# Two of three convolution taps on GpSimd, V shifted by DMA, and loads issued from two queues

## The chip, the cores and the metric

The kernel runs on one core of one Trainium2 chip. The metric is the device time of one execution in microseconds (us), as the median of several runs. The engines are TensorE (PE in the profile, with its weight loads as PEld), VectorE (DVE), ScalarE (ACT), GpSimd (POOL) and SyncE (SP, which here only issues DMAs). Each engine works through its own instructions in a fixed order.

## The reference

Sliding-window attention over 8 batches of 8 heads, 576 positions and 64 elements, then a feed-forward part with a gated three-tap convolution along the sequence:

```python
def _attn_ref(q, k, v):                       # B=8, H=8, S=576, D=64
    scores = scale * np.matmul(q, k.transpose(0, 1, 3, 2))
    mask = np.abs(pos[:, None] - pos[None, :]) <= 32
    ...                                       # masked softmax
    return np.matmul(attn, v)

def _moe_ref(x, w_in, conv_w, w_out):         # d_model=512, d_ff=1024
    h = np.maximum(x @ w_in, 0.0)
    ...                                       # hp: h padded by one row at each end
    for k in range(3):
        conv_out += conv_w[k][None, None, :] * hp[:, k:k + S, :]
    gate = 1.0 / (1.0 + np.exp(-conv_out))
    return h * gate @ w_out
```

## The kernel before

The rows of all batches are cut into 12 chunks of 384 and the 1024 hidden features into 8 blocks of 128. One (chunk, block) pair is a unit: a projection into PSUM on TensorE, ReLU on ScalarE, three convolution taps, tanh on ScalarE, the gate on VectorE. A tap on TensorE is a matmul with a diagonal matrix; in 79 units the middle tap is instead multiplied and added into PSUM by VectorE.

```python
        on_dve = m < P["tap"][c]
        kks = (0, 2) if on_dve else (0, 1, 2)

        def emit_pc(e_):
            for kk in kks:
                tensor.matmul(pc.ap[:, 0:nc_], diag_w[:, kk, m, :], taps(kk), start=(kk == 0), stop=(kk == 2))
# ... cut ...
            def emit_tap(e_):
                vector.scalar_tensor_tensor(
                    out=in3(pc.ap), in0=taps(1), scalar=conv_w_sb[:, 1, m:m + 1], in1=in3(pc.ap),
                    op0=ALU.mult, op1=ALU.add,
                )
```

All large loads are issued by SyncE: four query and key loads of 576 KB per batch (two groups of heads each), five V loads of 192 or 256 KB, and two loads for each weight matrix.

```python
        def emit(e):                                   # load_qk
            src = (q, k)[y][b, 4 * i:4 * i + 4, :, :]
            sync.dma_start(
                s.ap[:, y].rearrange("p e j d -> p e (j d)"),
                bass.AP(src.tensor, src.offset, [[RP * D, 128], [2 * S * D, 2], [1, RP * D]]),
            )
# ... cut ...
        def emit_hi(e):                                # shift_v: V moved by 64 rows, on VectorE
            mover(e, vo[0:64, c0:c1], ve[64:128, c0:c1])
```

The order of instructions on each engine is not written by hand. The program holds a planner: it simulates the engines with given costs and given priorities (the dictionary `P`, found by a search over many plans) and emits each engine's instructions in the order that its simulation gives. So the times in `P` fit one plan, and a part moved by hand leaves every other instruction where the plan had put it.

The softmax here doesn't subtract the row's maximum and nothing guards it: scores larger than these inputs give would overflow.

## Time and profile before

| | before |
|---|---|
| time, median of the 3 runs | 236.06 us (234.93 to 236.89) |
| span of the profiled execution | 234.2 us |
| first projection matmul starts | 24.6 us |
| from there to the end | 209.6 us |
| TensorE, VectorE, ScalarE, GpSimd busy | 219.8, 197.5, 181.6, 62.8 us |

I take as the end of the start the first matmul of the projection `pf<-xT,w_in_sb`, because from there the feed-forward work can fill TensorE. The view of the tile w_in_sb gives it; its columns are shortest, median and longest duration in ns, then the start of the first and of the last.

```profile
L380 PE MATMUL pf<-xT,w_in_sb x416: 243/327/338, 24.6 to 223.4; 128*128 128x385 bf16 x88, 128*128 128x386 bf16 x30, 128*128 128x193 bf16 x21
```

The window of the first 24 us (window, length, busy time and count of PE, PEld, DVE, ACT and POOL, granted clock, DMA share, GB/s) shows DMA engines nearly full:

```profile
0.00:24.00 24.00, 18.06 (x301) 12.38 (x302) 17.89 (x60) 16.09 (x41) 10.81 (x40) 1.00 0.98 295
```

### The profile page before, as it was taken

The numbers are of one execution on the slowest core, as the hardware profiler recorded it, in microseconds if no ns is written. First come the engines' busy times: TensorE is split into PE (matmuls) and PEld (weight loads), VectorE is DVE, ScalarE is ACT, GpSimd is POOL, SyncE is SP. The second block draws the span as 40 slices with busy tenths as digits, with TensorE's granted clock in tenths as the row PEclk, the third lists the DMA queues.
The fourth block names the chain that finished last, engine by engine and source line by source line (L and its number), as shares of the span: only waits on it lengthen the run. The fifth ranks groups of instructions, "written<-read, shape, count | busy, mean of one in ns | idle before, by whom it ended". The sixth has DMA issues, their size and how long they took to land.

```text
span 234.2 us, 7175 instructions
## 1 busy us (share of the span) xinstructions
PE 219.8 (94%) x2790; PEld 128.5 (55%) x2790; DVE 197.5 (84%) x463; ACT 181.6 (78%) x432; POOL 62.8 (27%) x101
## 2 busy tenths in 40 slices
PE   7777999899999899999999999999999999999992
PEld 4555556578555555655555555555555655555550
DVE  6489989896999999999999999887997995867271
ACT  3796989999999697798689687797599855766361
POOL 4336655552733531152360210340000000000000
PEclk9999999999999999999999999999999999999999
DMA  6999999999999988649995994981442143211204
GB/s 219 294 261 393 284 264 299 359 201 379 201 321 326 243 273 242 153 55 264 372 196 60 253 186 119 328 219 46 69 75 99 48 88 102 92 45 45 91 3 179
DMA packets 66054, 45.37 MB, mean 194 GB/s; under 512 B 51148, under 2 KB 51172, under 8 KB 66020
## 3 DMA queue, kind: packets, MB, share of 16 engines
q1 hardware_dynamic: 65984, 44.90, 71.1%
q8 instruction: 22, 0.36, 0.8%
q14 instruction: 12, 0.10, 0.1%
q10 hardware_dynamic: 36, 0.01, 0.0%
HBM read 32.52 MB, written 9.44 MB: 179 GB/s over the span
## 4 chain that ended last, share of the span: by engine, by line
PE 65%; DVE 19%; ACT 5%; DMA 3%; issue 3%; SPq 1%; ACTq 0%; POOL 0%; DVEq 0%; POOLq 0%
PE pf L380 65%; DVE gT L380 5%; DVE attn L380 4%; DMA vst<-in_v_dram 3%; DVE pf L380 3%; DVE diag_w L380 3%; ACT attn L380 2%; DVE vo L380 2%; DVE xn L380 1%; SPq L380 1%; ACT pf L380 1%; ACT xn L380 1%; DVE rec L380 1%; DVE qkT L380 1%; DVE xT L380 1%
## 5 line engine op out<-in xcount | busy, mean ns | idle before, releaser
L380 PE MATMUL pf<-xT,w_in_sb 128*128 128x385 bf16 (+2 forms) x416 | 73.9, 315 | 1.4 <-DVE gT L380 0.9
L380 PE MATMUL pf<-w_out_sb,gT 128*128 128x512 bf16 x288 | 67.8, 379 | 0.1
L380 ACT ACTIVATE pf<-pf 128x384 f32<-128x384 f32 (+1 forms) x104 | 47.0, 478 | 13.1 <-DVE pf L380 12.3
L380 ACT ACTIVATE hT<-pf 128x385 bf16<-128x385 f32 (+2 forms) x104 | 48.1, 501 | 11.3 <-PE pf L380 10.1
L380 DVE SCALAR_TENSOR_TENSOR gT<-pf,hT 128x384 bf16<-128x384 f32 (+1 forms) x104 | 51.4, 519 | 5.9 <-ACT pf L380 5.3
L380 DVE SCALAR_TENSOR_TENSOR pf<-hT,conv_w_sb,pf 128x384 f32<-128x384 bf16 x79 | 46.0, 616 | 11.4 <-PE pf L380 10.3
L380 PEld LDWEIGHTS <-w_in_sb 128*128 128x128 bf16 x416 | 38.8, 98 | 24.9 <-issue 2.7
L380 PE MATMUL pf<-hT,diag_w 128*128 128x384 bf16 (+1 forms) x233 | 46.3, 310 | 0.7 <-DVE gT L380 0.3
L380 POOL TENSOR_SCALAR qkb<-st 128x1152 bf16<-128x1152 f32 (+1 forms) x27 | 29.6, 1097 | 57.2 <-DMA st<-in_q_dram 30.5
L380 PEld LDWEIGHTS <-gT 128*128 128x128 bf16 x288 | 27.4, 98 | 29.7 <-ACT attn L380 0.3
L380 ACT ACTIVATE attn<-pf 128x512 bf16<-128x512 f32 (+1 forms) x96 | 41.0, 528 | 2.1 <-PE pf L380 1.9
L380 POOL TENSOR_SCALAR ve<-vst 128x512 bf16<-128x512 f32 x37 | 25.0, 682 | 30.4 <-DMA vst<-in_v_dram 24.6
L380 DVE TENSOR_TENSOR attn<-attn,mask 128x1152 bf16<-128x1152 bf16 x32 | 27.5, 859 | 5.2 <-ACT attn L380 4.8
L380 ACT COPY y<-pf 128x512 f32<-128x512 f32 x32 | 19.5, 612 | 11.1 <-PE pf L380 7.4
L380 PEld LDWEIGHTS <-diag_w 128*128 128x128 bf16 x233 | 19.8, 97 | 13.2 <-issue 0.8
L380 ACT COPY qkT<-pf 128x576 bf16<-128x576 bf16 x36 | 22.7, 660 | 1.8 <-PE pf L380 1.7
L380 DVE TENSOR_TENSOR xn<-pf,rec 128x256 bf16<-128x256 f32 x64 | 23.4, 408 | 0.1
L380 DVE COPY qkT<-pf 128x576 bf16<-128x576 bf16 x28 | 20.4, 748 | 2.9 <-PE pf L380 2.3
L380 DVE COPY vo<-ve 64x520 bf16<-64x520 bf16 (+1 forms) x28 | 15.4, 549 | 2.0 <-POOL ve L380 1.2
L380 PEld LDWEIGHTS <-attn 128*64 128x64 bf16 x576 | 11.8, 110 | 9.4 <-issue 5.7
L380 PE MATMUL pf<-ve,attn 128*64 128x65 bf16 x320 | 15.0, 197 | 2.1 <-DVE attn L380 1.2
L380 PE MATMUL pf<-qkT 64*128 64x64 bf16 x576 | 14.3, 191 | 1.6 <-DVE qkT L380 0.9
(39 smaller groups left out, 139.4 us busy)
## 6 DMA issues: line engine op xcount, KB each, us to landing
st<-in_q_dram SPq DMA_DIRECT2D x16, 576.0 KB, 6.7
st<-in_k_dram SPq DMA_DIRECT2D x16, 576.0 KB, 7.2
out_dram<-y SPq DMA_DIRECT2D x36, 256.0 KB, 2.4
vst<-in_v_dram SPq DMA_DIRECT2D x24, 256.0 KB, 8.5
vst<-in_v_dram SPq DMA_DIRECT2D x16, 192.0 KB, 7.5
st<-in_moe_w_in_dram SPq DMA_DIRECT2D x2, 1024.0 KB, 7.1
st<-in_moe_w_out_dram SPq DMA_DIRECT2D x2, 1024.0 KB, 7.8
xT<-xn SPq DMA_TRANSPOSE x30, 2.5
```

The source lines that it names most:

```text
L380: return lambda *args, **kwargs: fixed(do(*args, **kwargs))
```

## The change

The intent is to relieve TensorE, which is busy 94% of the span: in some units no tap is left on it, GpSimd makes two of them in fp32 SBUF, and VectorE adds the third and writes PSUM. To pay for this, VectorE loses its large V shifts to DMA, and GpSimd loses the query and key casts of batches 2 to 7. The query and key loads of batches 0 and 1 go to ScalarE's queue, beside SyncE's. The planner gets a model of two queues, and all of `P` is searched anew. The core of the diff, with cuts:

```diff
+    PLANS = {
+        "3": ((0, 1, 2), (), ()), "2": ((0, 2), (), (1,)), "1": ((0,), (), (1, 2)),
+        "q": ((), (0, 2), (1,)), "r": ((), (0,), (1, 2)), "s": ((0,), (1, 2), ()),
+    }                                        # taps on TensorE, on GpSimd, on VectorE
 ...
+        def emit_mul(e_, cp, kk):
+            gpsimd.tensor_scalar(
+                out=in3(cp.ap), in0=taps(kk), scalar1=w_tap(kk), scalar2=0.0, op0=ALU.mult, op1=ALU.add
+            )
+        def emit_add(e_):
+            gpsimd.tensor_tensor(out=in3(cps[0].ap), in0=in3(cps[0].ap), in1=in3(cps[1].ap), op=ALU.add)
 ...
+        def emit_tap(e_, kk, from_):
+            vector.scalar_tensor_tensor(
+                out=in3(pc.ap), in0=taps(kk), scalar=w_tap(kk), in1=in3(from_.ap), op0=ALU.mult, op1=ALU.add,
+            )
 ...
+    queue = {"SP": sync, "ACT": scalar}
-            sync.dma_start(
+            queue[e].dma_start(              # in every load; also in mover, for the shift of V
 ...
- 'e_vo': (('DVE',), ('DVE',), ('DVE',)),
+ 'e_vo': (('DVE',), ('DVE',), ('SP',)),
- 'e_qk': (('POOL', 'DVE', 'ACT'), ('POOL',), ('POOL', 'ACT')),
+ 'e_qk': (('POOL', 'ACT'), ('POOL', 'DVE', 'ACT'), ('DVE', 'ACT')),
+ 'q_qk': ('ACT', 'ACT', 'SP'),
+ 'q_v': (('SP', 'SP', 'SP', 'SP', 'SP'), ('SP', 'SP', 'SP', 'SP', 'ACT'), 'SP'),
+ 'q_w_in': 'SP',
+ 'kind': ('33333333', '33333333', '2q222222', '22qq2q2q', '22qq212q', '2q2q2222', 'q2222q22', '2qsq222q', '222q2q2q',
+          'qs222q22', '22q12q2q', 'q2sr2q2q'),
```

## The prediction

> **What bounds the kernel now.** I read the page's shares first, then the chain that ended last, then busy time by stage, then the groups of instructions with what they waited for. The page:
>
> ```profile
> PE 219.8 (94%) x2790; PEld 128.5 (55%) x2790; DVE 197.5 (84%) x463; ACT 181.6 (78%) x432; POOL 62.8 (27%) x101
> ...
> PE 65%; DVE 19%; ACT 5%; DMA 3%; issue 3%; SPq 1%; ACTq 0%; POOL 0%; DVEq 0%; POOLq 0%
> ```
>
> TensorE is busy 94% and carries 65% of the chain that ended last; VectorE carries 19%; GpSimd, idle for 73% of the span, none. The chain in order of time shows where: its late part is one unbroken TensorE piece.
>
> ```profile
> 3.60 7.82 DMA vst<-in_v_dram
> ...
> 24.21 5.16 DVE diag_w L380 x15
> 29.89 9.18 PE pf L380 x167
> ...
> 145.21 15.12 PE pf L380 x189
> 160.35 0.60 ACT attn L380
> 160.95 0.38 ACT pf L380
> 161.33 0.52 ACT attn L380
> 161.85 0.04 issue
> 161.90 67.35 PE pf L380 x589
> ```
>
> So there are three stages: a start that waits for loads and then for VectorE (to about 24 us), a middle in which TensorE and VectorE alternate in the chain, and from about 145 us a stage that TensorE alone sets. Busy time in the last two:
>
> ```profile
> 24.00:150.00 126.00, 122.19 (x1730) 73.20 (x1729) 117.09 (x272) 108.21 (x263) 48.78 (x56) 1.00 0.93 242
> 150.00:229.00 79.00, 78.91 (x761) 42.84 (x759) 61.80 (x132) 56.24 (x127) 3.21 (x5) 1.00 0.31 85
> ```
>
> The columns are window, length, then busy time (and count) of PE, PEld, DVE, ACT and POOL, granted clock, DMA share, GB/s. In the middle VectorE is at 117.1/126 = 93%, almost as full as TensorE. In the last stage TensorE has 78.9 of 79 us, VectorE 78%, ScalarE 71%, GpSimd 4%. That contrast decides my numbers: a TensorE instruction saved late is worth its full time, one saved in the middle only a part.
>
> The groups that the change touches:
>
> ```profile
> L380 PE MATMUL pf<-hT,diag_w 128*128 128x384 bf16 (+1 forms) x233 | 46.3, 310 | 0.7 <-DVE gT L380 0.3
> L380 DVE SCALAR_TENSOR_TENSOR pf<-hT,conv_w_sb,pf 128x384 f32<-128x384 bf16 x79 | 46.0, 616 | 11.4 <-PE pf L380 10.3
> L380 POOL TENSOR_SCALAR qkb<-st 128x1152 bf16<-128x1152 f32 (+1 forms) x27 | 29.6, 1097 | 57.2 <-DMA st<-in_q_dram 30.5
> L380 DVE COPY vo<-ve 64x520 bf16<-64x520 bf16 (+1 forms) x28 | 15.4, 549 | 2.0 <-POOL ve L380 1.2
> ```
>
> The first is the convolution on TensorE: 233 diagonal matmuls. The second is the middle tap, which 79 units already leave to VectorE. The 310 ns of one matmul is latency, not cost: in the timeline five of them begin at 183.43 us and the next operation at 184.25 us, so one costs 0.82/5 = 0.164 us of TensorE.
>
> **What the Trainium skill says.** "TensorE: Matmul & The Clock Gate", the section "Wait — 56ns, not 53.3ns?", gives start to start as N/2.4 GHz plus about 2.5 ns; for 384 columns that is 0.1625 us, and the trace's 0.164 agrees. "GPSIMD Engine Reference", section 3.1, gives about 2.6 cycles per element for a two-input operation at 1.2 GHz and about one for a light one-input body. The trace has no two-input GpSimd operation; its one-input casts agree (1152 elements 1.151 us, 512 elements 0.621 us by their medians: 0.83 ns, one cycle, per element, and 0.2 us fixed). "SBUF — State Buffer", the section "SBUF: two separate sides", says that VectorE and GpSimd share a port pair under an exclusive lock, for VectorE operations with two SBUF inputs or in a 2-port mode. The trace agrees in kind: the mask multiply takes 0.758 us in the median and 1.484 at most, the shift copies of V stretch to 1.533. "DMA: Bandwidth & Descriptors", the section "Issuing engines are not separate DMA queues", says that a second issuing engine saves only issue time; this trace, with nearly all traffic on one queue, can't show it.
>
> **The change part by part.** The new plan string gives each unit of chunks 2 to 11 a kind. I count 26 q (two taps on GpSimd, none on TensorE), 3 s (one tap on TensorE, two on GpSimd, a plain add on VectorE), 1 r (one tap on GpSimd, two on VectorE), 2 "1" (one on TensorE, two on VectorE) and 48 "2", the present split; chunks 0 and 1 keep three taps on TensorE.
>
> TensorE. Those 80 units use 48*2 + 2*1 + 3*1 = 101 matmuls, against 79*2 + 3 = 161 now. Sixty go: 60 * 0.164 = 9.8 us. By chunk 2 to 11 the sixty lie 2, 8, 7, 4, 4, 7, 7, 5, 7, 9. The last stage begins with some 5.3 chunks left (42 of VectorE's gate operations lie in it, 8 to a chunk), so about 36 of the sixty fall in it: 5.9 us. The other 24 are in the middle: 3.9 us.
>
> GpSimd. A multiply of 384 elements by the casts' line is 0.2 + 384*0.83 ns = 0.52 us; an add, estimated from the skill's 2.6 cycles, 0.2 + 384*2.17 ns = 1.03 us. A q or s unit costs 2*0.52 + 1.03 = 2.07 us; 29 of them and one lone multiply make 60.6 us. From it go the query and key casts of batches 2 to 7, no longer allowed there: about 20 of the 23 large ones at 1.15 us, 23 us. GpSimd ends near 62.8 + 60.6 - 23 = 100 us, under half the span.
>
> VectorE. In a q unit one operation (middle tap plus GpSimd's sum, into PSUM) replaces the present tap, and in an s unit a plain add does: I count both as 0.616 us, no change. The r, the two "1" and the one unit that had three TensorE taps add about four operations, 2.5 us. The 12 large shift copies of batches 2 to 7 become DMAs: minus 12 * 0.795 (the large form's mean) = 9.5 us. Against that, the 24 casts of batches 2 to 7 now go to VectorE or ScalarE. Split evenly, that is 12 on ScalarE at 1.16 us (its mean for this form), 14 us, of which some 6 are there already, and 12 on VectorE at, as an estimate from the mask's 0.726 us best case for the same length, 0.7 us: 8.4 us. ScalarE does eight normalizations of the first batches in 32 pieces; in batch 0 they may now go to VectorE only, at most eight times 0.41 = 3.3 us. The sum is +4.7 us, to about 202, before locks. Those are the sore point: GpSimd now reads SBUF in the late stage as well, and some 85 VectorE operations (32 masks, 29 new taps, a dozen casts, remaining shifts) can meet it. With GpSimd busy 45% and a mean remainder of 0.4 us, an unplanned meeting costs 0.18 us on average, up to 15 us in all; the schedule plans around part of it. I take 6 us, giving about 208.
>
> Start. Query and key loads of batches 0 and 1 go to ScalarE's queue while V stays on SyncE's. Now SyncE is held 8.33 us issuing the first five V loads, and the chain runs through them (7.82 us). But DMA engines are 98% busy in the first 24 us, so the second queue reorders bytes more than it adds any. I give it 0.
>
> The sum: late stage 5.9 us, of which I keep 5.2 (locks and thinner slack cost a little); middle 3.9 us, of which I keep 2.1, because VectorE there loses shifts but gains casts and meetings; start 0. 236.06 - 7.3 = 228.8 us, 3.1% less.
>
> **The rivals.** First, *VectorE takes TensorE's place.* At 208 of 229 us it would be 91% busy, and in the middle it is at 93% already. For it: 19% of the chain is VectorE today, and ScalarE already waits 12.3 us for the taps. Against it: the late stage has 17 us of VectorE slack in 79. If only the late gain survives, 231 us; if meetings cost all that I feared, 233 to 235.
>
> Second, *GpSimd's latency becomes a wait.* A q unit's chain after its ReLU grows by 2.07 us, with two scratch buffers, one unit ahead at best, and the in-order GpSimd queue also holds V casts that wait for their loads (24.6 us of such waits now). A late load then holds up a tap, a tanh and a gate. For it: every queue has a fixed order. Against it: most waiting before V casts lies in the middle, 3.3 us of it after 150. It would cost 2 to 4 us: 231 to 233.
>
> Third, *all of it is kept.* The two queues smooth the loads, shifts leave VectorE's critical moments, and the whole 9.8 us plus 1 to 3 us at the start come out: 223 to 226 us. For it: the entire schedule was retuned with the change. Against it: the tail of about 5 us after the last matmul and DMA-bound start stay.
>
> **Range and chances.** 228.8 us is the sum above; 224.5 is the third rival's middle, 233.5 the first's worse half. The 2% line is 231.3 us, 2.5 us above my figure, and the late gain alone nearly reaches it. Faster by over 2%: 0.69; within 2%: 0.28; slower by over 2%: 0.03.
>
> **What would show it.** Diagonal matmuls should number 173, and TensorE's busy time fall to about 206 to 211 us. GpSimd should be near 100 us with some 59 multiplies of 0.5 us and 29 adds of 1.0 us; no large shift copy on VectorE; V shifts as twelve DMAs; casts of queries on VectorE or ScalarE after batch 1. If VectorE carries clearly over 19% of the chain, or its two-SBUF-input operations grow well past their medians, the first rival has it; if taps wait for GpSimd by many microseconds, the second. My prediction is wrong if the span after 150 us shrinks by less than 4 us, or if the start changes by more than 2 us either way.

## More of the kernel before

ScalarE's timeline at the start follows: start, duration, engine, instruction, and in brackets the idle time before it and what ended it. ACTq is the issue of a DMA.

```profile
0.80 0.65 ACTq L380 DMA_DIRECT2D conv_w<-in_moe_conv_w_dram  x1
1.48 1.28 ACT L380 ACT_TABLE_LOAD   x1 [1.48 <-PEq L1010]
5.02 0.73 ACT L380 CAST qkb<-st 128x640 bf16<-128x640 f32 x1 [2.27 <-DMA st<-in_q_dram]
```

ScalarE issues one small load, loads its table, and casts the first query at 5.02 us, as soon as it has landed.

## The result, and the profile after

The changed kernel takes 243.44 us (median of four runs, 241.67 to 244.91); the kernel before, beside it, 235.68 us (four runs). The ratio is 1.0321, with a 95% interval of 1.0235 to 1.0408: slower, where I had predicted 228.8 us. A ratio here is the mean time of one kernel's fast runs over that of the other's in the same rounds, so it is not quite the ratio of the medians quoted beside it. Executions over 1.5% slower than the fastest of the same kernel are left out of the means.

The page of the changed kernel, busy times and chain:

```profile
PE 213.7 (88%) x2692; PEld 125.6 (52%) x2715; DVE 192.9 (80%) x475; ACT 190.0 (78%) x427; POOL 101.9 (42%) x160
...
PE 39%; DVE 23%; ACT 20%; DMA 7%; issue 6%; POOL 2%; SPq 0%; ACTq 0%; DVEq 0%; POOLq 0%
```

TensorE and VectorE both have less work than before, and yet the span is 8.1 us longer. TensorE's share of the chain fell from 65% to 39%, while VectorE's rose from 19% to 23% and ScalarE's from 5% to 20%. The tile view says where it begins:

```profile
L445 PE MATMUL pf<-xT,w_in_sb x416: 244/327/338, 38.6 to 229.7; 128*128 128x385 bf16 x88, 128*128 128x386 bf16 x30, 128*128 128x193 bf16 x21
```

The first projection starts at 38.6 us instead of 24.6, 14.0 us later. The windows from there to the end, before and then after:

```profile
24.60:234.20 209.60, 201.26 (x2485) 115.83 (x2484) 178.98 (x402) 164.92 (x391) 51.62 (x61) 1.00 0.69 182
```

```profile
38.60:242.30 203.70, 189.76 (x2260) 109.72 (x2281) 170.08 (x401) 168.95 (x388) 83.84 (x113) 0.99 0.70 183
38.60:166.00 127.40, 119.93 (x1613) 71.73 (x1625) 109.89 (x270) 115.47 (x269) 43.98 (x61) 0.99 0.89 232
166.00:234.00 68.00, 66.92 (x637) 36.87 (x646) 58.94 (x130) 52.17 (x118) 39.87 (x52) 1.00 0.38 102
```

So the start is 14.0 us longer, the rest 209.6 - 203.7 = 5.9 us shorter, and 14.0 - 5.9 = 8.1. TensorE's busy time in the rest fell by 11.5 us, at nearly the same clock. The last two lines answer to the prediction's middle and late stage: TensorE still fills the late one (66.9 of 68 us), VectorE is at 87% in it where it was at 78%, and GpSimd at 59% where it was at 4%.

These two numbers are not a pure loss and a pure gain, because the mark cuts the work at different places. The windows of TensorE's score matmuls, which read the tile qkT, from 0 to the first projection (before, then after; busy time and count, clock, DMA share, GB/s):

```profile
0.00:24.60 24.60, 1.79 (x72) 1.00 0.99 297
0.00:38.60 38.60, 4.76 (x144) 0.78 0.96 291
```

One batch has 576/8 = 72 of them. The transposes of queries and keys stand at 72 and 144 as well. So the new plan puts the front of batch 1's attention, 144 matmuls, ahead of the first projection: that work has moved from the rest into the start. At full clock it keeps TensorE busy some 5.9 us (10.2 us for both groups in run b below against 4.3 in run d, which has them once).

What the parts of the change became stands in the groups of instructions of the changed kernel (busy us and mean ns of one after the bar, then idle time before them and what ended it):

```profile
L445 POOL TENSOR_SCALAR cp<-hT,conv_w_sb 128x384 f32<-128x384 bf16 x59 | 39.1, 672 | 56.5 <-ACT hT L445 43.2
...
L445 PE MATMUL pf<-hT,diag_w 128*128 128x384 bf16 (+1 forms) x173 | 34.1, 306 | 3.6 <-ACT hT L445 2.6
...
L445 POOL TENSOR_TENSOR cp<-cp,cp 128x384 f32<-128x384 f32 x29 | 28.9, 998 | 2.0
...
L445 DVE TENSOR_TENSOR attn<-attn,mask 128x1152 bf16<-128x1152 bf16 x32 | 24.8, 777 | 1.6 <-ACT attn L445 1.6
...
L445 DVE SCALAR_TENSOR_TENSOR pf<-hT,conv_w_sb,cp 128x384 f32<-128x384 bf16 x27 | 17.4, 644 | 6.2 <-POOL cp L445 3.1
```

There are 173 diagonal matmuls, 59 multiplies and 29 adds, as counted from the plan string. VectorE's taps that read GpSimd's sum waited only 3.1 us for it. The mask multiply, which has two SBUF inputs and can meet GpSimd, takes 777 ns in the mean.

The start is read from ScalarE's timeline in the changed kernel:

```profile
1.45 0.41 ACTq L445 DMA_DIRECT2D st<-in_q_dram  x1
...
3.12 0.99 ACTq L445 DMA_DIRECT2D st<-in_k_dram  x1
7.50 0.38 ACTq L445 DMA_DIRECT2D st<-in_q_dram  x1
7.91 0.48 ACTq L445 DMA_DIRECT2D st<-in_k_dram  x1
9.36 0.38 ACTq L445 DMA_DIRECT2D st<-in_q_dram  x1
13.21 0.37 ACTq L445 DMA_DIRECT2D st<-in_k_dram  x1
13.62 1.28 ACT L445 ACT_TABLE_LOAD   x1 [13.62 <-DMA vst<-in_v_dram]
14.91 0.62 ACT L445 CAST qkb<-st 128x512 bf16<-128x512 f32 x1
```

The first four loads (batch 0) go out in 0.4 to 1.0 us each. The next four (batch 1) go out at 7.50, 7.91, 9.36 and 13.21 us, and each of the gaps ends when an earlier load has landed: GpSimd's casts of batch 0's first query and key, which wait for their loads, start at 7.56 and 9.42 us, and the chain has a V load under way from 1.84 us for 11.35 us, to 13.19. In the program's own instruction list these issues carry a wait: every load counts up one of eight completion counters, taken in turn by the loads of both queues, and a load waits until the eighth load before it has landed. ScalarE executes in order, so these waits hold back its computing too: its first cast runs at 14.91 us and not at 5.02. The list of waits has it in two places, first the hold, then TensorE behind the cast:

```profile
ACT L445 <- DMA vst<-in_v_dram: 13.6, 1, 13.6
...
PE pf L445 <- ACT qkb L445: 10.4, 1, 10.4
```

The columns are the total, the number of times and the longest wait. The second queue moved no more bytes: in the same first 24 us as above the transfer rate is 292 GB/s, against 295, while every engine did about half to four fifths of the work.

```profile
0.00:24.00 24.00, 11.99 (x162) 7.53 (x163) 9.35 (x40) 8.63 (x15) 9.12 (x34) 0.72 0.93 292
```

SyncE's timeline of the changed kernel shows the third thing: with batch 1's queries and keys already under way, w_in is issued at 17.61 us, where the kernel before, which sends w_in ahead of batch 1, issues it at 11.98.

### The profile page after: what moved, and what is told of

Same layout as the page of the kernel before. It is cut to its first block, busy times and chain, and to the rows that moved or that the text cites.

```text
span 242.3 us, 7092 instructions
## 1 busy us (share of the span) xinstructions
PE 213.7 (88%) x2692; PEld 125.6 (52%) x2715; DVE 192.9 (80%) x475; ACT 190.0 (78%) x427; POOL 101.9 (42%) x160
## 4 chain that ended last, share of the span: by engine, by line
PE 39%; DVE 23%; ACT 20%; DMA 7%; issue 6%; POOL 2%; SPq 0%; ACTq 0%; DVEq 0%; POOLq 0%
PE pf L445 39%; DMA vst<-in_v_dram 7%; ACT attn L445 6%; DVE pf L445 5%; DVE gT L445 4%; ACT hT L445 4%; ACT pf L445 4%; DVE attn L445 4%; DVE xn L445 3%; ACT qkT L445 3%; DVE qkT L445 2%; DVE vo L445 2%; POOL cp L445 2%; ACT y L445 1%; DVE rec L445 1%
## 5 line engine op out<-in xcount | busy, mean ns | idle before, releaser
L445 POOL TENSOR_SCALAR cp<-hT,conv_w_sb 128x384 f32<-128x384 bf16 x59 | 39.1, 672 | 56.5 <-ACT hT L445 43.2
L445 POOL TENSOR_SCALAR ve<-vst 128x512 bf16<-128x512 f32 x31 | 20.2, 657 | 55.2 <-DMA vst<-in_v_dram 28.2
L445 PE MATMUL pf<-hT,diag_w 128*128 128x384 bf16 (+1 forms) x173 | 34.1, 306 | 3.6 <-ACT hT L445 2.6
L445 DVE SCALAR_TENSOR_TENSOR pf<-hT,conv_w_sb,pf 128x384 f32<-128x384 bf16 x53 | 31.5, 616 | 6.4 <-PE pf L445 5.3
L445 POOL TENSOR_TENSOR cp<-cp,cp 128x384 f32<-128x384 f32 x29 | 28.9, 998 | 2.0
L445 ACT COPY qkT<-pf 128x576 bf16<-128x576 bf16 x39 | 25.4, 710 | 1.8 <-PE pf L445 1.8
L445 DVE TENSOR_TENSOR xn<-pf,rec 128x256 bf16<-128x256 f32 x69 | 25.2, 410 | 0.1
L445 PE MATMUL pf<-ident,qkb 64*128 64x64 bf16 x576 | 14.4, 195 | 10.6 <-ACT qkb L445 10.4
L445 ACT CAST qkb<-st 128x1152 bf16<-128x1152 f32 (+2 forms) x21 | 23.1, 1109 | 0.0
L445 DVE SCALAR_TENSOR_TENSOR pf<-hT,conv_w_sb,cp 128x384 f32<-128x384 bf16 x27 | 17.4, 644 | 6.2 <-POOL cp L445 3.1
L445 PEld LDWEIGHTS <-diag_w 128*128 128x128 bf16 x173 | 14.8, 97 | 12.3 <-issue 3.5
```

Source lines behind the costliest of these rows:

```text
L445: return lambda *args, **kwargs: fixed(do(*args, **kwargs))
```

## The experiments

**Theory 1**, at first: ScalarE's held-up computing is the cost of the start (most of the 14 us), and undoing it gives the time back. **Rival 1**: two queues share the same DMA engines, so every urgent load lands later, whoever issues it. **Rival 2**: the order of the bytes is the cost, batch 1's four loads (4 * 576 KB = 2.36 MB) ahead of V's last blocks and of w_in; at 295 GB/s they are worth some 8 us, as an estimate from the window above. All twelve kernels gave correct results. The ratios and medians use fast runs alone; slow ones were one of six of h, one of four of k, one of 17 of l, and four of the 11 of the kernel before beside h, i and j. The fast median of the kernel before, run beside each, was 235.56 us for a to d, 234.56 for e to g, 234.58 for h to j, 234.69 for k and 234.76 for l. The table gives for each profiled execution the two parts of the span, and how many matmuls of batch 1's attention (transposes and scores) stand ahead of the first projection.

| run | first projection, us | batch 1's matmuls ahead | from there to the end, us | median us | ratio to before (95%) |
|---|---|---|---|---|---|
| before | 24.6 | 0 | 209.6 | 235.68 | 1 |
| after | 38.6 | 144 | 203.7 | 243.44 | 1.0321 (1.0235 to 1.0408) |
| a_one_queue | 32.2 | 144 | 205.4 | 238.49 | 1.0115 (1.0054 to 1.0175) |
| b_four_on_act | 36.1 | 144 | 203.4 | 241.13 | 1.0208 (1.0143 to 1.0272) |
| c_one_queue_replan | 25.2 | 0 | 232.5 | 258.38 | 1.0959 (1.0875 to 1.1043) |
| d_before_act | 27.8 | 0 | 209.9 | 239.70 | 1.0162 (1.0108 to 1.0215) |
| e_before_late_w_in | 31.1 | 108 | 208.3 | 240.88 | 1.0257 (1.0199 to 1.0314) |
| f_taps_on_pe | 31.3 | 144 | 229.3 | 261.62 | 1.1125 (1.1048 to 1.1201) |
| g_shift_on_dve | 31.4 | 144 | 213.0 | 245.86 | 1.0467 (1.0410 to 1.0524) |
| h_taps_one_queue | 25.2 | 0 | 206.3 | 232.40 | 0.9878 (0.9809 to 0.9948) |
| i_taps_one_queue_2 | 25.7 | 0 | 203.7 | 230.09 | 0.9792 (0.9719 to 0.9866) |
| j_no_taps | 27.4 | 0 | 209.0 | 238.32 | 1.0169 (1.0083 to 1.0255) |
| k_held_back | 36.8 (slow run) | 144 | 207.3 (slow run) | 241.54 | 1.0294 (1.0240 to 1.0348) |
| l_best_four_on_act | 29.9 | 0 | 204.1 | 235.98 | 1.0056 (1.0029 to 1.0082) |

### a_one_queue: the changed kernel, every load issued by SyncE

```diff
-    queue = {"SP": sync, "ACT": scalar}
+    queue = {"SP": sync, "ACT": sync}
```

> The changed kernel with its plan untouched, but every load issued by SyncE. Theory 1 (ScalarE's queue is held by its eight load issues, the last of which goes out at 13.2 us, so its first cast comes at 14.9 us instead of 5.0): ScalarE's first cast by about 6 us, first projection matmul at 25 to 29 us instead of 38.6, clock back to about 1.00, time 229 to 233 us. Rival 1 (the two queues share the DMA engines, so query and key loads land later): the same recovery here; the next run tells them apart. Rival 2 (the loss lies in GpSimd taps, locks and the rest of the schedule, and the late start is caught up with anyway): 240 us or more.

The time fell to 238.49 us, and the first projection came at 32.2 us: 6.4 of the 14.0 us, not all of it; both are outside what theory 1 and rival 1 had put down. Only the queue was changed here, so the second queue, with the hold and the sharing together, costs the changed kernel 243.44 - 238.49 = 5.0 us. ScalarE's first cast ran at 6.55 us, so the hold is gone and a further cause is left. Every load keeps its place in the plan's order, and that order has batch 1's four loads ahead of V's last three blocks. Those blocks are cast at 19.3 to 21.6 us here, and at 13.8 to 17.8 in the kernel before; w_in is issued at 18.16. But no load stands in the chain between 9.1 us and the first projection. What stands there first is TensorE's work:

```profile
9.82 9.51 PE pf L445 x132
```

What follows, up to 29.9 us, is mostly VectorE's attention work. So the chain points to the order of computing, with batch 1's 144 matmuls ahead of the first projection, more than to the loads. From 10 to 20 us TensorE was busy all the time at a granted clock of 0.52. In f and g, whose start is the same program, the clock was 1.00 there and the first projection came at 31.3 and 31.4 us: by that the low clock cost some 0.9 us of a's start, as an estimate.

### b_four_on_act: only batch 0's queries and keys stay on ScalarE

```diff
-            queue[e].dma_start(                                    # load_qk
+            (queue[e] if b == 0 else sync).dma_start(
-            queue[e].dma_start(                                    # load_v
+            sync.dma_start(
```

> The changed kernel with its plan untouched; only the four query and key loads of batch 0 stay on ScalarE's queue, those of batch 1 and the one V load go to SyncE. Theory 1: the four issues go out without a long wait, so ScalarE casts by 7 to 8 us, first projection matmul before 31 us, 231 to 235 us. Rival 1 (sharing): the loads of V and of batch 0 still run side by side, query and key still land at 7.5 to 13 us, time stays at 238 us or more.

ScalarE is free after its four issues, at 4.23 us, and yet the time is 241.13 us. Its timeline shows why:

```profile
4.23 1.28 ACT L445 ACT_TABLE_LOAD   x1 [4.23 <-issue]
7.70 0.62 ACT L445 CAST qkb<-st 128x512 bf16<-128x512 f32 x1 [2.19 <-DMA st<-in_q_dram]
...
10.70 0.73 ACT L445 CAST qkb<-st 128x640 bf16<-128x640 f32 x1 [1.00 <-DMA st<-in_k_dram]
...
13.71 0.72 ACT L445 CAST qkb<-st 128x640 bf16<-128x640 f32 x1 [0.50 <-DMA st<-in_q_dram]
...
16.72 0.72 ACT L445 CAST qkb<-st 128x640 bf16<-128x640 f32 x1 [0.92 <-DMA st<-in_k_dram]
```

Each of the casts waits for its load. The loads land every 3.0 us, until 16.7 us, where on one queue the same plan (a) has GpSimd's casts of the same loads at 6.6, 9.2, 10.6 and 12.1 us, and the kernel before, which loads nothing in between, ScalarE's at 5.0, 6.5, 8.5 and 10.3 us. This is rival 1's picture, not theory 1's. SyncE's timeline shows what they share with: two of V's loads, and then batch 1's queries and keys, issued at 1.84 to 7.70 us.

The clock is no explanation of the whole: in the changed kernel it was 0.50 between 10 and 20 us, while here the profile has 0.999 over the span and the first projection still starts at 36.1 us. But it adds something (see a), and the profile of the changed kernel had the low clock where that of b had not.

### c_one_queue_replan: one queue, and the planner plans again

```diff
- 'q_qk': ('ACT', 'ACT', 'SP'),
- 'q_v': (('SP', 'SP', 'SP', 'SP', 'SP'), ('SP', 'SP', 'SP', 'SP', 'ACT'), 'SP'),
+ 'q_qk': ('SP', 'SP', 'SP'),
+ 'q_v': (('SP', 'SP', 'SP', 'SP', 'SP'), ('SP', 'SP', 'SP', 'SP', 'SP'), 'SP'),
```

> The changed kernel with all loads planned for SyncE, so that its own planner makes a new order for one queue. Theory 1: start as in the kernel before (first projection matmul 24 to 28 us), 229 to 233 us. Rival 2: 240 us or more.

The start is back: 25.2 us. The planner, given one queue, puts V and w_in ahead of batch 1 by its priorities. But the rest grew to 232.5 us, for the other numbers of `P` had been fitted to another plan: the chain now holds single waits such as 10.34 us for a V shift by DMA. The time lies in the range put down for rival 2, though the start does not bear it out. As a test of the start it counts, with the limit that the planner moved batch 1's computing back along with its loads; as a test of the time it doesn't.

### d_before_act: the kernel before, with two queues

```diff
-            sync.dma_start(                                        # load_qk
+            (scalar if b < 2 else sync).dma_start(
```

> The kernel before, plan untouched, with the query and key loads of batches 0 and 1 issued by ScalarE: four ahead of its first cast, four later in its order, each of those where the plan has it. Theory 1: the four first cost little, the later ones hold ScalarE for the time that their slot waits last, 1 to 4 us in all: 236 to 240 us. Rival 1: query and key of batch 0 land after 7.5 us instead of 4.9, start later by 3 us or more: 239 us or more, with ScalarE's first cast waiting for the load and not for an issue.

The time rose to 239.70 us, within theory 1's span, but by rival 1's mechanism. The first casts of ScalarE come at 7.78, 9.75 and 11.71 us instead of 5.02, 6.47 and 8.47, and before the first of them the engine waited for the load. The first projection is 3.2 us later. So the second queue costs the untouched kernel about 3 us at the start. A held issue stands in this chain too (batch 1's last load, at 23.54 us), so it is not sharing alone; l below is the cleaner test.

### e_before_late_w_in: the kernel before, w_in behind batch 1

```diff
- 'w_in': (-99.0, -98.9),
+ 'w_in': (-89.9, -89.85),
```

> The kernel before, one queue, with one number changed, so that its planner loads the first weight matrix behind the query and key loads of batch 1, as the changed kernel does. Theory (the order of the loads is the larger half of the late start): first projection matmul at 29 to 33 us instead of 24.6, 239 to 244 us. Rival (only the second queue matters): first projection matmul by 26 us, 235 to 238 us. The planner makes a new order for the rest as well, so the first projection matmul counts for more than the time.

By its numbers a hit for rival 2: one queue, no second issuer, the first projection at 31.1 us (6.5 later) and the time 2.6% longer. The chain says less. Its last pieces before the first projection are

```profile
28.35 2.19 ACT attn L380 x5
30.54 0.51 ACT w_in_sb L380
```

ScalarE's cast of w_in stands behind ScalarE's own attention work; GpSimd's cast that waited for the last half of w_in began at 29.04 us, and no load is in the chain after 8.4 us. The planner had made a new order for the computing as well, with 108 of batch 1's matmuls ahead of the first projection where the kernel before has none. So the run shows that this plan starts late; it does not separate the order of the loads from that of the computing.

### f_taps_on_pe and g_shift_on_dve: what the taps and the shifts are worth

Both start from a_one_queue. The first puts GpSimd's 59 taps back on TensorE just ahead of VectorE's operation; the second makes the twelve large V shifts on VectorE again.

```diff
+                for x in on_pool:                                  # f, in emit_tap and emit_sum
+                    tensor.matmul(
+                        pc.ap[:, 0:nc_], diag_w[:, x, m, :], taps(x), start=(x == on_pool[0]), stop=(x == on_pool[-1])
+                    )
```

> The one-queue run (238.5 us) with its plan untouched, but the 59 taps of GpSimd computed by TensorE as diagonal matmuls just ahead of the VectorE operation that used them; GpSimd's multiplies and adds are gone. Theory (the taps' removal shortens the part after the first projection by 5 to 7 us because TensorE bounds it): 59 * 0.164 = 9.7 us of TensorE come back, 243 to 248 us, first projection matmul unchanged at 32 us. Rival (VectorE or its meetings with GpSimd bound it, so the taps bought nothing): 236 to 240 us.

```diff
-        if e in queue:                                             # g, in mover
-            queue[e].dma_start(out_, in_)
-        else:
-            copier(e, out_, in_)
+        copier("DVE" if e in queue else e, out_, in_)
```

> The one-queue run (238.5 us) with its plan untouched, but the twelve large V shifts made by VectorE copies again instead of DMAs. Theory (VectorE, 80% busy, isn't the bound; the shift DMA's longer way is hidden too): 237 to 240.5 us. Rival (VectorE bounds the middle, so 12 * 0.8 = 9.5 us come back there): 243 us or more. A third possibility, that the shift DMAs wait behind loads and hold up TensorE: 235.5 us or less.

Run f took 261.62 us, far above what either side expected. The matmuls stand in TensorE's in-order queue at places where no plan had put them, and VectorE's taps then wait 32.1 us for TensorE. I count it as inconclusive.

Run g took 245.86 us, and the rest of its span is 213.0 us against 205.4: 7.6 us lost, where VectorE got 12 copies of some 0.8 us, 9.5 us by the kernel before's mean. Here the theory put down for the run fell and the rival to it was right: in this plan VectorE, at 182.0 of 213.0 us, was not the busiest engine, and yet most of the addition counted. As in f, the copies stand where no plan had put them, so this is their price in a foreign plan. I had booked the shifts as bookkeeping for VectorE's balance.

### h, i and j: planned for one queue, with GpSimd's taps and without

To separate the taps from the loads, I planned the changed kernel again. The planner learned the wait that the traces show, loads all go to SyncE with w_in right behind batch 0, the shifts stay on VectorE, and `P` was searched anew. h and i are two outcomes of that search from different starting points (64 and 59 GpSimd multiplies); j is the control, the same planner and search without GpSimd's taps.

```diff
-                        if o.dma and rings.room(e) < o.dma[0] / 16.0:
+                        if o.dma and (rings.room(e) < o.dma[0] / 16.0
+                                      or (len(sent) >= 8 and sent[-8] is not None and sent[-8] not in landed)):
...
+ 'e_vo': (('DVE',), ('DVE',), ('DVE',)),
+ 'q_qk': ('SP', 'SP', 'SP'),
```

> The changed kernel's code, replanned: every load on SyncE, the first weight matrix loaded right behind batch 0, a planner that lets no load be issued while the eighth one before it is under way, V shifts on VectorE, GpSimd taps in chunks 0 to 11 (parameters searched anew with the planner). Theory (the taps themselves are worth some 6 us and the start cost 14): first projection matmul at 24 to 26 us, 226 to 231 us, faster than both kernels. Rival (what GpSimd saves TensorE is lost in meetings with VectorE and waits for its chain): 234 us or more.

> As the run before, from another starting point of the search, so that the spread between such plans is seen: theory 226 to 232 us, rival 234 us or more.

> The control: the same code, planner, search and one queue, but no unit may use GpSimd; taps lie on TensorE and VectorE alone. Theory: 3 to 6 us slower than the two runs with taps, 230 to 236 us. Rival (the new search, not the taps, makes the gain): within 2 us of them.

They took 232.40, 230.09 and 238.32 us, beside 234.58 for the kernel before. Run i lies in the theory's range; h is slower than its range, and j slower than its own. Run i beats both kernels: 0.9792, interval 0.9719 to 0.9866, clear of 1 but not of the 2% line. The busy line of its page and that of the control's, one after the other:

```profile
PE 212.8 (93%) x2723; PEld 125.3 (55%) x2745; DVE 206.3 (90%) x494; ACT 177.0 (77%) x418; POOL 115.2 (50%) x178
```

```profile
PE 221.7 (94%) x2787; PEld 132.0 (56%) x2812; DVE 208.2 (88%) x490; ACT 176.5 (75%) x409; POOL 71.4 (30%) x126
```

TensorE has 8.9 us less work with the taps (i against j), and the time is 5.9 (h) to 8.2 us (i) shorter. Not all of that is the taps. The control, at 1.0169, is slower than the kernel before, which has no GpSimd taps either, so planner and search alone can be worth some 4 us, and there is one control only. In the rest, where all four have none of batch 1's matmuls moved ahead, h has 206.3 and i 203.7 us against 209.0 for the control and 209.6 for the kernel before: 2.7 to 5.9 us less. Beside the changed kernel, i has the same rest, 203.7 us, and starts its projection at 25.7 us instead of 38.6; the difference of 12.9 us is the whole difference of their spans, 242.3 - 229.4. As i has none of batch 1's front in its start, it does more work in that same rest.

### k_held_back: two queues, batch 1's loads behind ScalarE's casts of batch 0

```diff
+    late_ = [x for x in order if x[2] == "ACT" and x[3].name in ("load q10", "load k10", "load q11", "load k11")]
+    order = [x for x in order if x not in late_]
+    last_ = max(n for n, x in enumerate(order) if x[2] == "ACT" and x[3].name[:7] in ("cast q0", "cast k0"))
+    order[last_ + 1:last_ + 1] = late_
```

> The changed kernel with both queues and its plan untouched, except that in ScalarE's order the four loads of batch 1 stand behind its four casts of batch 0 instead of ahead of everything. Theory (ScalarE is held by load issues that wait for earlier loads to land): its first cast at 7 to 8 us instead of 14.9, first projection matmul at 31 to 36 us instead of 38.6, 236 to 241 us. Rival (the issues only seem to hold it; the casts would have waited for their data anyway): first cast after 12 us, 242 us or more.

This takes away the hold and keeps the two queues. The first cast ran at 7.00 us instead of 14.91, and the time was 241.54 us in the median of its three fast runs (the profiled one slow). The first cast is where the theory had it; the time is just above its range. The ratio, 1.0294, can't be told from the changed kernel's 1.0321. Here w_in is issued at 10.35 us, ahead of batch 1's loads, and the first projection still comes at 36.8 us: sending w_in first did not help here, where the engines' orders still have batch 1's front ahead of it. The wait moved: the loads now go out at 13.6 us and later, and ScalarE's first large cast of batch 1 waits for them:

```profile
26.09 1.15 ACT L445 CAST qkb<-st 128x1152 bf16<-128x1152 f32 x1 [5.61 <-DMA st<-in_q_dram]
```

### l_best_four_on_act: the best kernel, with batch 0's queries and keys on ScalarE

```diff
-            queue[e].dma_start(                                    # load_qk, in i_taps_one_queue_2
+            (scalar if b == 0 else sync).dma_start(
```

> The fastest kernel so far (ratio 0.979 to the kernel before), its plan untouched, with only the four query and key loads of batch 0 issued by ScalarE, side by side with SyncE's V loads. Theory (two queues share the DMA engines, so the loads that the start needs first land some 3 us later; nothing holds ScalarE long): first query cast at 7 to 8 us instead of 5, first projection matmul 2.5 to 5 us later than 25.7, ratio 0.990 to 1.005. Rival (the second queue as such is harmless, only the eight issues and the order of the loads hurt): ratio within 0.975 to 0.985.

Measured with many rounds: 1.0056 (1.0029 to 1.0082), where i alone has 0.9792. So the second queue costs the best kernel about 2.6%. Its first query cast is at 7.30 us instead of 4.82, and its first projection 4.2 us later. There is no hold here, and only four loads were moved: of all runs this is nearest to sharing alone. The ratio lies a hair above the theory's span and far from the rival's.

## Why the prediction was wrong

**The start.** The step that failed is "But DMA engines are 98% busy in the first 24 us, so the second queue reorders bytes more than it adds any. I give it 0." Its premise was right, 292 GB/s against 295, and its conclusion was not: reordering is worth nothing only if it does not matter which bytes come late. With the plan untouched, the second queue cost 5.0 us of time (a), and the first projection came 14.0 us later, in place of 0. By the ladder of runs, each step one edit further from the changed kernel, the 14.0 us part as follows:

- 2.5 us (38.6 to 36.1, changed kernel to b) with ScalarE's hold removed, the difference of the clocks included. Run k, which removes it in another way, gives back 0.3% of the time, which is less than its uncertainty. The wait that stands out most in the profile, TensorE 10.4 us behind ScalarE's cast, was worth a quarter of its length or less, because the loads behind it land late as well.
- 3.9 us (36.1 to 32.2, b to a) with the second queue removed. In the best kernel, where nothing is held, it costs 4.2 us at the start (l). The Trainium skill, "DMA: Bandwidth & Descriptors", section "Queues, rings and completion order", says that each DMA engine takes packets in turn from the queues that have work. Batch 0's queries and keys, which must come first, then share with loads that are not needed yet (V's and, in b, batch 1's); the casts 3.0 us apart in b agree with that, though no run looks inside a DMA engine.
- 7.6 us (32.2 to 24.6, a to before) are left, and here the cause is not isolated. The plan has batch 1's loads ahead of V's last blocks and of w_in, and batch 1's 144 matmuls ahead of the first projection. All runs without those matmuls ahead start at 24.6 to 29.9 us, all with them (108 in e) at 31.1 to 38.6. The chains of a and e hold computing and no load there, and k, with w_in sent ahead of batch 1, starts at 36.8 us (a slow run). That speaks for the order of computing; but no run with one queue changes the order of the loads and keeps that of the computing.

Not all of the 7.6 us is lost, because the moved work is missing from the rest: run a as a whole is 238.49 - 235.56 = 2.9 us slower than the kernel before.

**The rest.** That fewer matmuls shorten it is borne out by h and i against their control, by 2.7 and 5.3 us, with the search's luck in these numbers. I took 7.3 us. In the changed kernel the rest is 5.9 us shorter, but batch 1's front, some 5.9 us of TensorE's busy time, has moved out of it, so this is no measure of the taps, and what they are worth there stays open. Even with one queue (a) that kernel gained nothing on the kernel before. Run i, with another plan and another start, comes out at 230.09 us, inside my range; that is not the plan that I predicted. Within the sum:

- The division into stages is not settled. By the prediction's own mark, 42 gate operations left, the late stage runs from 149.8 us to the end before and from 164.1 after, which is 84.4 and 78.2 us: 6.2 us gained, a little more than the 5.2 that I kept, and nothing in the middle, where I kept 2.1, although batch 1's front had left it. By the mark of 42 ReLUs left (146.3 and 157.6 us) it is 3.2 and 2.7 us. One reason may be that a unit takes longer from ReLU to gate with GpSimd in between; that was not measured.
- The counts held: 173 matmuls, 59 multiplies, 29 adds. TensorE's busy time over the span, 213.7 us, missed "about 206 to 211" because of the start: after the first projection it fell by 11.5 us, but the part before it took 23.9 us instead of 18.5, with batch 1's front in it and the clock at 0.50 from 10 to 20 us.
- GpSimd's cost was close: the add 0.998 us for an estimate of 1.03, the multiply 0.588 us in its median for 0.52 (0.672 in the mean), and 101.9 us in all for 100.
- VectorE was sized in the wrong direction: 192.9 us for 208. Of 6 us for lock meetings nothing is seen on VectorE, as the mask multiply went from 859 ns in the mean to 777 (GpSimd's multiplies are longer in the mean than in the median by 84 ns, 59 * 0.084 = 5.0 us in all, which may be meetings from the other side); only 9 of the query and key casts came to VectorE, not 12; and building the diagonal matrices took 4.6 us instead of 7.9.
- The shifts of V were worth more than I said. Run g has 7.6 us for them in that plan. That is the price in a plan made without them; i, planned with them on VectorE, has a rest of 203.7 us all the same. How the gain divides between taps and shifts in the changed kernel itself stays open, because f, which should have told, disturbed the plan too much.

**The rivals.** The first, VectorE as the bound, is not clearly ruled out: VectorE's share of the chain rose to 23%, the prediction's own sign for it, and g shows how near it is; but its busy time fell, and its two-input operations did not grow. The second, waiting for GpSimd, is small: VectorE waited 3.1 us for it in all, and GpSimd has 2% of the chain. The third expected the two queues to smooth the loads and was wrong in sign. None of the three asked what a later landing does to the first batch, and so the 0.03 for slower was far too low. My own last test did name it: "or if the start changes by more than 2 us either way".

## What to carry to other kernels

While the DMA engines are full, ask of each load which computation waits for it and send the bytes in that order; here a second queue brought no more bytes (292 and 295 GB/s) and urgent loads landed later (l, d). Before issuing loads from an engine that computes, look for what an issue may itself wait, because everything behind it on that engine waits too. And when a change has several parts, measure the start and the rest apart, as a good part can hide behind a bad one; but check first that the same work lies on each side of the mark, which it did not here.

## What the Trainium skill lacked or had wrong

- "DMA: Bandwidth & Descriptors", section "Issuing engines are not separate DMA queues": right that a second issuer brings no bandwidth (292 and 295 GB/s). It says that all of them interleave, but not that this can delay an urgent load: first query cast at 7.78 us for 5.02 (d) and at 7.30 for 4.82 (l); these kernels took 1.6% and 2.6% longer.
- The same section speaks only of the sequencer time that is saved. It lacks the cost on an engine that computes: an issue waiting for earlier loads to land held ScalarE's first cast until 14.91 us, instead of 5.02.
- "SBUF — State Buffer", section "SBUF: two separate sides", gives the lock but nothing from which to tell how often two operations meet, and I took 6 us for it. The runs show no clear growth with GpSimd's load: the mask multiply's mean was 859 ns with GpSimd busy 27% (before), 872 at 30% (j), 777 at 42% (after), 805 at 50% (i) and 907 at 57% (h).
- "GPSIMD Engine Reference", section 3.1: its 2.6 cycles for a two-input add held (0.998 us for 384 elements, estimate 1.03). The multiply by a scalar from bf16 into fp32 came to 0.588 us in the median for 384 elements, more than the 0.52 us that I had taken from casts.
